# Fewer, wider stores of the last output tile and another order in the head of a fused attention and ELU kernel

## Chip, cores and metric

One core of a Trainium2 chip runs the whole kernel as one program. The metric is the device time of one execution in microseconds (us). Five engines work side by side, each through its own list of instructions in order: TensorE (PE, with its weight loads as PEld), VectorE (DVE), ScalarE (ACT), GpSimd (POOL) and SyncE (SP). SP and ACT also issue the DMA transfers; in the profile SP's transfers are queue q1 and ACT's are queue q10. Engines wait for each other, and for transfers, through semaphores.

## Reference

Inputs: `q`, `k`, `v` of shape (4 batches, 4 heads, 1088 positions, 32), two sketches `S1`, `S2` of shape (8, 32), and the weights `w_in` (128, 2048) and `w_out` (2048, 128), all given in 64-bit floats that the kernel rounds to float32 itself where it needs them (the sketches and the weights; `q`, `k`, `v` are float32).

```python
def phi(x):
    a = np.einsum('rd,bhsd->bhsr', S1, x)
    b = np.einsum('rd,bhsd->bhsr', S2, x)
    return np.einsum('bhsi,bhsj->bhsij', a, b).reshape(*x.shape[:-1], r * r)
q_p, k_p = phi(q), phi(k)
kv  = np.einsum('bhsf,bhsd->bhfd', k_p, v)
z   = np.sum(k_p, axis=2)
num = np.einsum('bhsf,bhfd->bhsd', q_p, kv)
den = np.einsum('bhsf,bhf->bhs', q_p, z)[..., None] + 1e-06
x   = (num / den) rearranged to (4352, 128)      # 4352 = 4 batches x 1088 positions, 128 = heads x 32
h   = x @ w_in
g   = np.where(h > 0, h, np.exp(np.minimum(h, 0)) - 1)
out = g @ w_out                                  # (4352, 128)
```

## The kernel before

**Tiling.** The 1088 positions of a batch are cut into 17 tiles of 64 (`NT` = 17, `KT` = 9), so there are 68 half tiles of 64 rows; a group `g` is 8 of them (512 columns), and the last of the nine groups has only 4. The 2048 hidden columns are 8 pairs `cp` of 2 x 128. The main loop walks over (group, pair): `mm1` makes two tiles of h on PE, `elu_a` (ACT, lines 787 and 789) and `elu_d` (DVE, line 795) make g, and `mm2`, `mm2_seven` or, for the last group, `mm2_last` adds the product with `w_out` up in PSUM. Between these steps the attention of the later batches is woven in by hand.

**Order.** The program is scheduled by hand: each engine runs its instructions in the order in which the Python code issues them. Only waits on semaphores come on top. Eight semaphores serve the DMA transfers in turn, so a transfer is issued once the one eight before it has landed.

**The head** (everything up to about 15 us) makes the first group's x from batch 0 as early as it can:

- Loads: `S1` on SP and `S2` on ACT (8 rows each), the first half of batch 0's keys (9 tiles) on SP and the second half (8 tiles) on ACT, the first 8 tiles of queries on SP, then on SP the first weights, `v` of batch 0 in two transfers, and the rest.
- `sps` (line 264) and `SXps` (`make_SXh`, line 250) on PE spread the two sketches; `Sab` (line 267, DVE) is `sps` times a mask of heads, the block matrix with which keys and queries are multiplied.
- `transp` (line 243) transposes keys and queries on DVE in 32 x 32 blocks: `kT` in four pieces (tiles 0 to 5 ahead of `Sab`, then 9 to 14, 5 to 9, 14 to 17), then `qT`.
- `KF(0)` (line 303) multiplies each `kT` tile with `Sab` into two PSUM tiles `abp`, in two streams, one for each half of the rows; two ACT copies (line 311) make `abk` of them. `q1_first` (line 478) does the same for the queries (`abqp`, copied to `abq` on ACT, line 482).
- The products of key features `kp` are made by POOL for tiles 0 to 4 (`KO_pool`, line 286) and by DVE for tiles 4 to 9 (`KO_first`, line 373).
- z: `z_tile` (line 381) sums over positions on PE (`zps`), `ZC` (line 403) copies to `zl` on ACT, `Z` (line 225) spreads on PE, and `Z_out` (line 412) masks on DVE into `SW`. `q1z_first` (line 490) multiplies the queries with it on PE (`zqp`), and `q2_den` (from line 565: `pw`, sum, reciprocal, `an`) and `q2_out` (line 582: `qp`, in two halves) finish the queries on DVE.
- `RA`, `RB`, `RC` round weights from 64-bit to 32-bit: `RA` (line 103) and `RC` (lines 116 to 129) on DVE, `RB` (line 108) on ACT.
- `KA(0)` (line 390) multiplies `v` with `kp` on PE; `KS_first` (lines 442 to 444) copies and transposes that; `q4_early` (line 594) transposes `qp` on PE, `q5_early` (line 601, `xps`) and the ACT copies at line 607 make `xg`, the x of a group.
- `keep_warm(n, cols)` (line 230) issues n products of constants into a PSUM tile that nobody reads. `KC` (line 399, `kvl`) copies kv out later, and line 225 is a helper that records most products, with `o` the result tiles of the first two groups.

**The tail.** `mm2_last` holds the last group's result with rows of the output on the partitions, in two PSUM tiles `ops[g][0]` and `ops[g][1]` (128 x 128 each, names `ol`). Tile i has half tile i on partitions 0 to 63 and half tile 2 + i on partitions 64 to 127. `fin_last` copies tile 0 on ACT and tile 1 on DVE (line 839) into `o`, and stores each half by itself (line 842): the lower half issued by SP, the upper by ACT. In `out`, the rows of one half tile lie 17 rows apart (64 rows of 512 bytes), and the two half tiles of a tile start two rows apart.

Of the kernel before, what the change touches and what calls it, by code (L numbers as in the profile page):

```python
# [22 lines left out]
def _ap(ap: bass.AP, free):  # L23
    return dataclasses.replace(ap, ap=[list(ap.ap[0])] + [list(x) for x in free])
# [3 lines left out]
def kernel(  # L28
# [21 lines left out]
    nc = tc.nc  # L50
# [7 lines left out]
    NT = S // 64  # L58
    KT = (NT + 1) // 2
# [12 lines left out]
    kT = [const.tile([FD, 2 * KT, 64], F32, name=f"kT{b}") for b in range(2)] * 2  # L72
    qT = [const.tile([FD, NT, 64], F32, name=f"qT{b}") for b in range(2)] * 2

    def load_hd(eng, x, src, b, t0, t1, c=slice(0, 2)):
        if (x, b) not in hd:
            hd[x, b] = work.tile([P, 2, NT, D], F32, name="hd_" + x, tag="hd_" + x)
        eng.dma_start(hd[x, b][:, c, t0:t1, :],
                      src[b].rearrange("h (a c t) d -> (h a) c t d", a=32, c=2)[:, c, t0:t1, :])
# [61 lines left out]
            eng.dma_start(S16[rs, :], src)  # L141
    load_hd(nc.sync, "k", k, 0, 0, KT)
    load_hd(nc.scalar, "k", k, 0, KT, NT)
    load_hd(nc.sync, "q", q, 0, 0, 8)
    warm = const.tile([R, 1], F32, name="warm")
    nc.vector.memset(warm[:], 0.0)
    nc.scalar.activation(warm[:], warm[:], EXP)
# [75 lines left out]
    def halves(dst, lhs, rhs, **kw):  # L223
        for u in range(2):
            nc.tensor.matmul(dst[64 * u:64 * u + 64], lhs[:, 64 * u:64 * u + 64], rhs, skip_group_check=True,  # L225
                             tile_position=(0, 64 * u), **kw)

    def keep_warm(n, cols=256):
        for i in range(n):
            nc.tensor.matmul(idle[:, :cols], some[:, :P], some[:, :cols], skip_group_check=True)  # L230
# [11 lines left out]
    def transp(dst, x, b, t0, t1):  # L242
        nc.vector.transpose(dst[b][:, t0:t1, :].rearrange("p t (a c) -> p c t a", c=2), hd[x, b][:, :, t0:t1, :])
# [4 lines left out]
    def make_SXh():  # L248
        xps = psum.tile([P, 512], F32, name="SXps", tag="aux")
        nc.tensor.matmul(xps[:, :FD], idr[:].rearrange("p x j -> p (x j)"), Sx[:].rearrange("p h d -> p (h d)"))  # L250
        nc.scalar.copy(SXh[:], xps[:, :FD])
        nc.gpsimd.tensor_mul(SXh[:].rearrange("p (h d) -> p h d", h=H), SXh[:].rearrange("p (h d) -> p h d", h=H),
                             _ap(hmask[:], [[1, H], [0, D]]))
# [9 lines left out]
    sps = psum.tile([P, 512], F32, name="sps", tag="aux")  # L263
    nc.tensor.matmul(sps[:, :2 * R], Sx[:].rearrange("p h d -> p (h d)"), ident[:, :2 * R])
    make_SXh()
    transp(kT, "k", 0, 0, 5)
    nc.vector.tensor_mul(Sab[:], _ap(sps[:, :2 * R], [[0, H], [1, 2 * R]]), _ap(bmask[:], [[1, H], [0, 2 * R]]))
    nc.gpsimd.tensor_copy(SW[:, :, :2, :].rearrange("p h x r -> p h (x r)"), Sab[:])

# [98 lines left out]
    def KO_first(t0, t1):  # L368
        half, o = divmod(t0, 5)
        n = t1 - t0  # L370
        a_ = kf_ps[half][:, 64 * o:64 * (o + n)].rearrange("p (m x r) -> p m x r", x=2, r=R)[:, :, 1, :]
        b_ = feats[0][:, 0, t0:t1].rearrange("p t h r -> p (t h) r")
        nc.vector.tensor_mul(feats[0, half][:, o:o + n].rearrange("p t h i j -> p (t h) i j"),
                             _ap(a_, list(a_.ap[1:]) + [[0, R]]), _ap(b_, [[R, n * H], [0, R], [1, R]]))
# [3 lines left out]
    def z_tile(b, ps, i):  # L378
        c = 32 * (i % 4)
        ab = feats[b]  # L380
        nc.tensor.matmul(ps[c:c + 32, R * R:R * R + H * R], ab[:, 0, i].rearrange("p h r -> p (h r)"),
                         ab[:, 1, i].rearrange("p h r -> p (h r)"), start=(b == 0 and i < 4), stop=(i >= KT - 4),
                         skip_group_check=True, tile_position=(0, c))
# [17 lines left out]
    def ZC(b, ps):  # L401
        zl = work.tile([P, H * R], F32, name="zl", tag="zl")
        nc.scalar.copy(zl[:], ps[:, R * R:R * R + H * R])
        return zl

    def Z(b, ps, zl):

        halves(ps[:, 96:128], SXh[:], zl[:])

    def Z_out(b, ps):  # L410
        z = wzs[b] = SW[:, :, 2, :] if b == 0 else work.tile([FD, H, R], F32, name="wz", tag="wz")[:]
        nc.vector.tensor_mul(z, ps[:, 96:128].rearrange("p (h i) -> p h i", h=H), _ap(bmask[:], [[1, H], [0, R]]))
# [21 lines left out]
    def Z_first():  # L434
        ps = psum.tile([P, 512], F32, name="zps", tag="h", bufs=4)
        for i in range(KT):
            z_tile(0, ps, i)
        return ps, ZC(0, ps)

    def KS_first():  # L440
        kd = work.tile([P, 2, R * R], F32, name="kd", tag="kd", bufs=1)
# [18 lines left out]
    def half_tile(g, k):  # L460
        return divmod(8 * g + k, NT)
# [11 lines left out]
    def q1_first():  # L473
        p = psum.tile([P, 512], F32, name="abqp", tag="aux")
        for i in range(4):
            for u in range(2):
                b, t = half_tile(0, 2 * i + u)
                nc.tensor.matmul(p[64 * u:64 * u + 64, i * 64:i * 64 + 64], qT[b][:, t, :],
                                 Sab[:].rearrange("p h y -> p (h y)"),
                                 skip_group_check=True, tile_position=(0, 64 * u))  # L480
        abw[0] = work.tile([P, H * 4, 2 * R], F32, name="abq", tag="abq", bufs=1)
        nc.scalar.copy(abw[0][:].rearrange("p (h t) y -> p h t y", h=H),
                       p[:, :256].rearrange("p (t h y) -> p h t y", t=4, h=H))

    def q1z_first():
        p = psum.tile([P, 512], F32, name="zqp", tag="h", bufs=4)
        for i in range(4):
            for u in range(2):
                b, t = half_tile(0, 2 * i + u)
                nc.tensor.matmul(p[64 * u:64 * u + 64, i * 32:i * 32 + 32].rearrange("p (h r) -> p h r", h=H),  # L490
                                 qT[b][:, t, :], SW[:, :, 2, :], skip_group_check=True, tile_position=(0, 64 * u))
        return p[:, :128].rearrange("p (t h r) -> p h t r", t=4, h=H)
# [341 lines left out]
    def fin_last():  # L834
        g, n = NQ - 1, qn[NQ - 1]
        o = work.tile([P, 2, P], F32, name="ol", tag="ol", bufs=1)
        rows = out.rearrange("(b y t) f -> b y t f", b=B, t=NT)
        for i, copy in enumerate((nc.scalar.copy, nc.vector.tensor_copy)):
            copy(o[:, i, :], ops[g][i][:])
            for u, eng in enumerate((nc.sync, nc.scalar)):  # L840
                b, t = half_tile(g, u * n + i)
                eng.dma_start(rows[b, :, t, :], o[64 * u:64 * u + 64, i])


    for t0, t1 in ((KT, KT + 5), (5, KT), (KT + 5, NT)):
        transp(kT, "k", 0, t0, t1)
    KF(0)
    transp(qT, "q", 0, 0, 8)
    zps, zl = Z_first()
    q1_first()  # L850
    KO_pool()
    KO_first(4, 5)
    KO_first(5, 7)
    Z(0, zps, zl)
    Z_out(0, zps)
    KO_first(7, KT)
    keep_warm(1, 96)
    zq = q1z_first()
    RA(0)
    q2_den(0, zq)  # L860
# [132 lines left out]
    for n in range(2, N + 2):  # L993
        if n < N:
            g, cp = steps[n]
# [26 lines left out]
        g, cp = steps[n - 2]  # L1022
# [5 lines left out]
        elif n > 2:  # L1028
            mm2(g, cp, cp == 0, cp == NP - 1)
            if cp == NP - 1:  # L1030
                fin1(g)
    fin_last()


# [27 lines left out]
```

## Time and profile before

| What | us |
|---|---|
| median of three runs | 267.58 |
| the three runs | 267.28, 267.58, 267.61 |
| the profiled execution: its own time | 267.61 |
| its span, first to last instruction | 265.83 |
| PE busy | 258.8 (97% of the span) |
| DVE, ACT, POOL busy | 187.8, 183.9, 159.8 |
| granted TensorE clock, mean | 1.000 of full speed |

All views count from the first instruction of the span. The time is 1.78 us longer than the span. The profile page has the busy times, the DMA queues with packets and bytes, and the chain of work that ended last, which is followed back from the last instruction. A timeline row gives start, length, engine, line, operation, output<-input, shapes and, in brackets, how long the engine was idle before it and who ended that; rows of one kind that follow each other closely are merged. In the records of DMA packets, each packet is one run of bytes that one of 16 DMA engines moved, without the name of that engine.

### The profile page before, as it was taken

How to read it: one execution, taken by the hardware profiler on the slowest of the kernel's cores; microseconds unless marked ns; L12 is line 12 of the kernel's file. 1: busy time of each engine (PE TensorE's matmuls, PEld its weight loads, DVE VectorE, ACT ScalarE, POOL GpSimd, SP SyncE). 2: the span in 40 equal slices, each digit the busy share in tenths (PEclk: the TensorE clock that was granted, in tenths of full speed). 3: DMA queues.
4: the chain of work that ended last, by engine and by line, in shares of the span. 5: the costliest groups of instructions: out<-in, count | busy, mean ns of one | idle time of the engine just before them, and what ended most of it. 6: DMA issues, size and time to landing. Idle time of an engine off the chain costs nothing.

```text
span 265.8 us, 7682 instructions
## 1 busy us (share of the span) xinstructions
PE 258.8 (97%) x3113; PEld 154.2 (58%) x3113; DVE 187.8 (71%) x347; ACT 183.9 (69%) x355; POOL 159.8 (60%) x233
## 2 busy tenths in 40 slices
PE   8799999999999999999999999999999999999994
PEld 7653233343334665668566666666766666666884
DVE  7899999996969796996557766654346444673652
ACT  2389978677566565786577777777777777777782
POOL 4400008204415985798858799898688888898300
PEclk9999999999999999999999999999999999999999
DMA  5999960010002300001100110001000100010011
GB/s 177 310 355 280 237 198 6 0 54 35 0 0 33 52 4 0 2 3 20 25 5 0 21 22 2 0 14 28 7 0 15 28 4 0 14 16 15 2 30 32
DMA packets 26402, 13.60 MB, mean 51 GB/s; under 512 B 19200, under 2 KB 24576, under 8 KB 26368
## 3 DMA queue, kind: packets, MB, share of 16 engines
q1 hardware_dynamic: 25920, 12.79, 19.1%
q8 instruction: 24, 0.39, 0.6%
q10 hardware_dynamic: 448, 0.33, 0.4%
q14 instruction: 10, 0.08, 0.1%
HBM read 10.88 MB, written 2.23 MB: 49 GB/s over the span
## 4 chain that ended last, share of the span: by engine, by line
PE 91%; ACT 4%; DMA 2%; SPq 1%; issue 1%; DVE 0%
PE h L225 42%; PE pb L726 16%; PE pa L726 12%; PE o L225 9%; PE ol L225 3%; DMA v<-in_v_dram 2%; PE kv L390 2%; PE h L644 1%; ACT e L789 1%; ACT e L787 1%; PE qps L644 1%; PE xps L601 1%; PE kfps L322 1%; PE qps L538 1%; PE kv L225 1%
## 5 line engine op out<-in xcount | busy, mean ns | idle before, releaser
L795 DVE SCALAR_TENSOR_TENSOR gg<-e,h 128x512 f32<-128x512 f32 (+1 forms) x144 | 92.3, 651 | 64.6 <-ACT e L789 63.2
L225 PE MATMUL h<-xg,W 128*64 128x512 f32 (+1 forms) x584 | 128.7, 563 | 0.0
L787 ACT ACTIVATE e<-h 128x512 f32<-128x512 f32 (+1 forms) x144 | 81.5, 566 | 50.4 <-PE h L225 47.9
L789 ACT ACTIVATE e<-e 128x512 f32<-128x512 f32 (+1 forms) x144 | 87.5, 607 | 4.4
L225 PEld LDWEIGHTS h<-xg,W 128*64 128x64 f32 x584 | 40.1, 137 | 47.4 <-issue 37.1
L706 POOL TENSOR_TENSOR tt<-gg 128x256 f32<-128x256 f32 x48 | 35.2, 733 | 16.4 <-DVE gg L795 15.9
L709 POOL TENSOR_TENSOR tt<-gg 128x256 f32<-128x256 f32 x48 | 35.4, 738 | 14.2 <-DVE gg L795 13.9
L711 POOL TENSOR_TENSOR tt<-gg,tt 128x256 f32<-128x256 f32 x48 | 36.5, 761 | 3.8
L710 POOL TENSOR_TENSOR tt<-tt,gg 128x256 f32<-128x256 f32 x48 | 35.2, 734 | 3.8
L726 PEld LDWEIGHTS pa<-gg,W 128*64 128x64 f32 x384 | 23.6, 137 | 22.8 <-issue 22.0
L225 PE MATMUL o<-gg,W 128*64 128x512 f32 x128 | 30.5, 598 | 0.2 <-ACT kvl L399 0.2
L726 PE MATMUL pa<-gg,W 128*64 128x128 f32 x384 | 29.5, 274 | 0.0
L726 PE MATMUL pb<-tt,SS 128*64 128x128 f32 x384 | 29.1, 273 | 0.0
L726 PEld LDWEIGHTS pb<-tt,SS 128*64 128x64 f32 x384 | 22.6, 137 | 0.0
L126 POOL TENSOR_TENSOR raw<-raw,tiny 128x512 f32<-128x512 f32 x1 | 1.0, 1042 | 30.4 <-DVE raw L121 30.4
L726 PE MATMUL pb<-gg,SS 128*64 128x128 f32 x192 | 18.7, 273 | 0.0
L726 PE MATMUL pb<-tt,W 128*64 128x128 f32 x192 | 18.6, 273 | 0.0
L726 PE MATMUL pa<-tt,SS 128*64 128x128 f32 x192 | 18.6, 273 | 0.0
L225 PEld LDWEIGHTS o<-gg,W 128*64 128x64 f32 x128 | 8.5, 136 | 16.2 <-issue 13.9
L726 PEld LDWEIGHTS pa<-tt,SS 128*64 128x64 f32 x192 | 12.1, 137 | 0.0
L726 PEld LDWEIGHTS pb<-tt,W 128*64 128x64 f32 x192 | 12.1, 137 | 0.0
L726 PEld LDWEIGHTS pb<-gg,SS 128*64 128x64 f32 x192 | 12.1, 137 | 0.0
(150 smaller groups left out, 242.2 us busy)
## 6 DMA issues: line engine op xcount, KB each, us to landing
raw<-in_moe_w_in_dram SPq DMA_DIRECT2D x8, 256.0 KB, 7.5
raw<-in_moe_w_out_dram SPq DMA_DIRECT2D x8, 256.0 KB, 7.0
hd_k<-in_k_dram SPq DMA_DIRECT2D x3, 544.0 KB, 8.3
hd_q<-in_q_dram SPq DMA_DIRECT2D x3, 544.0 KB, 9.1
v<-in_v_dram SPq DMA_DIRECT2D x4, 288.0 KB, 8.8
out_dram<-ob SPq DMA_DIRECT2D x72, 16.0 KB, 1.5
v<-in_v_dram SPq DMA_DIRECT2D x4, 256.0 KB, 7.7
out_dram<-ob SPq DMA_DIRECT2D x16, 32.0 KB, 1.7
```

What stands on the lines that cost most here:

```text
L225: nc.tensor.matmul(dst[64 * u:64 * u + 64], lhs[:, 64 * u:64 * u + 64], rhs, skip_group_check=True, tile_position=(0, 64 * u), **kw)
L322: nc.tensor.matmul(ps[g2][32 * c:32 * c + 32, :32 * KT], Sxp[r].rearrange("p x c r -> p (x c r)"), kT[b][r, u * KT:u * KT + KT, 32 * w:32 ...
L390: nc.tensor.matmul(kv[32 * h:32 * h + 32, :R * R], vt[b][:, (h * KT + i) * D:(h * KT + i + 1) * D], kp[i // 5][:, i % 5, h].rearrange("p i ...
L644: nc.tensor.matmul(ps[w][s * r:s * r + s, 64 * k:64 * (k + m)], lhs, qpT[g, i][rows, o + 2 * k:o + 2 * (k + m), f, :], start=(f == 0 and j ...
L706: nc.gpsimd.tensor_tensor(t[:, 0], b12, b11, op=SUB)
L709: nc.gpsimd.tensor_tensor(t[:, 2], b22, b12, op=SUB)
L710: nc.gpsimd.tensor_tensor(t[:, 1], t[:, 2], b11, op=ADD)
L711: nc.gpsimd.tensor_tensor(t[:, 3], b21, t[:, 1], op=SUB)
L726: nc.tensor.matmul(bank[64 * u:64 * u + 64, P * col:P * col + P], lhs, rhs[:, u], start=(first and i in (0, 3)), stop=last, skip_group_che ...
L787: nc.scalar.activation(e, hs[g, cp][c][:, :n], RELU, scale=-1.0)
L789: nc.scalar.activation(e, e, EXP, scale=-1.0)
L795: nc.vector.scalar_tensor_tensor(gs[g, cp][:, c, :n], es[g, cp][:, c, :n], -1.0, hs[g, cp][c][:, :n], op0=ADD, op1=MAX)
```

## The change

Head: q's first load is split into two transfers, c = 0 on SP and c = 1 on ACT (behind ACT's half of the keys). The first piece of `kT` is transposed behind `Sab` in place of ahead of it, and a filler product of 224 columns stands on PE behind `SXps`. z's sums, copy, spread and mask are issued together, after `q1_first` and after all of `KO_first`; `KO_first(5, 7)` and `KO_first(7, KT)` become one instruction `KO_first(5, KT)`. The filler after z has 160 columns in place of 96.

Tail: each of the two last tiles is stored by one transfer of 128 rows, tile 0 issued by ACT behind its copy, tile 1 by SP behind the copy on DVE. On the DRAM side the transfer is written as (u, y, f) = 2 x 64 x 128: u steps from a half tile to the one two rows on, y over its 64 rows.

The function that loads half heads takes a slice of c already:

```python
    def load_hd(eng, x, src, b, t0, t1, c=slice(0, 2)):
        ...
        eng.dma_start(hd[x, b][:, c, t0:t1, :],
                      src[b].rearrange("h (a c t) d -> (h a) c t d", a=32, c=2)[:, c, t0:t1, :])
```

```diff
     load_hd(nc.sync, "k", k, 0, 0, KT)
     load_hd(nc.scalar, "k", k, 0, KT, NT)
-    load_hd(nc.sync, "q", q, 0, 0, 8)
+    load_hd(nc.sync, "q", q, 0, 0, 8, slice(0, 1))
+    load_hd(nc.scalar, "q", q, 0, 0, 8, slice(1, 2))
...
     make_SXh()
-    transp(kT, "k", 0, 0, 5)
+    keep_warm(1, 224)
     nc.vector.tensor_mul(Sab[:], ...)
...
     def Z_first():
         ps = psum.tile([P, 512], F32, name="zps", tag="h", bufs=4)
         for i in range(KT):
             z_tile(0, ps, i)
-        return ps, ZC(0, ps)
+        zl = ZC(0, ps)
+        Z(0, ps, zl)
+        Z_out(0, ps)
+        keep_warm(1, 160)
...
     def fin_last():
...
-        for i, copy in enumerate((nc.scalar.copy, nc.vector.tensor_copy)):
+        for i, (copy, eng) in enumerate(((nc.scalar.copy, nc.scalar), (nc.vector.tensor_copy, nc.sync))):
             copy(o[:, i, :], ops[g][i][:])
-            for u, eng in enumerate((nc.sync, nc.scalar)):
-                b, t = half_tile(g, u * n + i)
-                eng.dma_start(rows[b, :, t, :], o[64 * u:64 * u + 64, i])
+            b, t = half_tile(g, i)
+            eng.dma_start(rows[b, :, t:t + n + 1:n, :].rearrange("y u f -> u y f"), o[:, i])
...
-    for t0, t1 in ((KT, KT + 5), (5, KT), (KT + 5, NT)):
+    for t0, t1 in ((0, 5), (KT, KT + 5), (5, KT), (KT + 5, NT)):
         transp(kT, "k", 0, t0, t1)
     KF(0)
     transp(qT, "q", 0, 0, 8)
-    zps, zl = Z_first()
     q1_first()
     KO_pool()
     KO_first(4, 5)
-    KO_first(5, 7)
-    Z(0, zps, zl)
-    Z_out(0, zps)
-    KO_first(7, KT)
-    keep_warm(1, 96)
+    KO_first(5, KT)
+    Z_first()
     zq = q1z_first()
```

## The prediction

> **What bounds the kernel now.** I read the chain of waits first, in two stretches, because the diff touches only the first 10 us and the last 4 us. In each row: start in us, length in us, what.
>
> ```profile
> 3.90 6.48 DMA v<-in_v_dram
> 10.38 0.14 issue
> 10.51 1.25 PE kv L390 x72
> ...
> 20.64 1.24 PE xps L601 x16
> 21.88 0.63 ACT xg L607 x2
> ...
> 30.42 0.27 ACT kvl L399
> 30.68 0.04 issue
> 30.73 1.50 PE o L225 x5
> ```
>
> To see: up to 10.38 us the end is set by the landing of `v`, not by the head's arithmetic; then PE and ACT pass the chain to and fro until 30.68, and from there PE is nearly unbroken. DVE, whose order the diff changes most, is nowhere on it. Next, the timeline of DVE in the head (start, length, engine, line, operation):
>
> ```profile
> 5.00 0.18 DVE L267 TENSOR_TENSOR Sab<-sps,bmask 128x64 f32<-128x64 f32 x1
> 7.08 1.11 DVE L373 TENSOR_TENSOR kp<-abp,abk 128x256 f32<-128x256 f32 x2 [0.17 <-ACT abk L311]
> 8.61 0.19 DVE L412 TENSOR_TENSOR SW<-zps,bmask 128x32 f32<-128x32 f32 x1 [0.42 <-PE zps L225]
> 8.71 0.68 DVE L373 TENSOR_TENSOR kp<-abp,abk 128x512 f32<-128x512 f32 x1
> 9.63 0.29 DVE L565 TENSOR_TENSOR pw<-abq,zqp 128x128 f32<-128x128 f32 x1
> ```
>
> The mask product of z (SW) starts at 8.61; `pw` follows 1.02 us later, through q1z. From 8.61 DVE has no idle stretch worth naming before 24.85, where it waits 0.34 us for ACT. So a late SW shifts DVE for 16 us; the question is who waits for DVE.
>
> Third, the timeline of the tail:
>
> ```profile
> 261.87 0.27 ACT L839 COPY ol<-ol 128x128 f32<-128x128 f32 x1 [1.06 <-PE ol L225]
> 262.16 1.19 SPq L842 DMA_DIRECT2D out_dram<-ol  x2
> 262.16 1.46 ACTq L842 DMA_DIRECT2D out_dram<-ol  x2
> 262.31 0.29 DVE L839 COPY ol<-ol 128x128 f32<-128x128 f32 x1 [1.04 <-PE ol L225]
> ```
>
> Issues start at 262.16 and 262.80 on SP, 262.16 and 262.81 on ACT. In the packet records SP's two transfers write at 263.36-263.66 and 264.00-264.30, ACT's at 263.63-263.93 and 264.28-264.59. The last instruction ends at 265.83, 1.24 us after the last packet, all of it waiting and closing.
>
> Fourth, the DMA queues (queue: packets, MB, share of 16 engines), once for 1.6:1.9, when only the sketches `S1` and `S2` are in flight, and once for 263.2:263.7, where q1 (SP) holds just the first output store:
>
> ```profile
> DMA packets 32, 0.00 MB, mean 14 GB/s; under 512 B 32, under 2 KB 32, under 8 KB 32
> ...
> q10 hardware_dynamic: 16, 0.00, 4.1%
> q1 hardware_dynamic: 16, 0.00, 4.0%
> ```
>
> ```profile
> q1 hardware_dynamic: 80, 0.03, 27.2%
> ```
>
> To see: a store of 64 rows leaves 80 packets, 64 of data and 16 completion records of 4 bytes: 16 engines took part. A sketch of 8 rows leaves 16, 8 of data and 8 completions: 8 engines. And both sketches used the same 8: the records pair off, such as data at 1.686 and completion at 1.698 on q1, then data at 1.710 and completion at 1.721 on q10, eight times over with the same 12 ns steps. So where the outermost count is below 16, it sets how many engines share a transfer, and two queues can land on the same ones.
>
> **The tail, step by step.** Four transfers become two. The built instruction has SBUF rows 128 x 128 on one side, and on the DRAM side the outermost count is 2 (2 x 64 x 128; the list of instructions shows 2x64x128 where it showed 64x128). The change removes one issue on SP (0.54) and one on ACT (0.81), each behind another, and SP's only one now waits for the DVE copy. No row here has unequal counts on its two sides. The bounds are 16 engines (the 64-row stores) and 2 (the destination's outer count); I take 2, nearest to the 8-row sketches, the only row with an outer count under 16.
>
> Rate of one engine: the share of 27.2% of 16 engines over 0.5 us is 2.18 us of packet time, less 16 x 9 ns of completions, over 64 packets: 32 ns per 512 bytes while 16 engines contend. The last engine of that store, alone by then, started packets at 263.554, .579, .604 and .628: 25 ns each. With two engines at work I take 25 and keep 32 for the range.
>
> The ACT store is issued at 262.16 as before; first packet 1.20 us later (SP's delay, both times): about 263.4. The DVE copy ends at 262.60, so SP issues at about 262.62 and is ready at 263.8, when the ACT store is a quarter done on the same two engines. Each engine has 64 + 64 packets: 128 x 25 ns = 3.2 us, done at 266.6 in place of 264.59: **+2.0 us**. At 32 ns: 4.1 us, done at 267.5, +2.9. On two separate pairs: 263.8 + 1.6 = 265.4, +0.85. What follows the last packet keeps its 1.24 us. Nothing hides this: only waiting comes after.
>
> The Trainium skill speaks on both sides. Its page DMA: Bandwidth & Descriptors, section Rules for kernel authors, advises one 128-partition transfer over two of disjoint halves, which is what the change does. The same page, section Why a DMA increments its semaphore by 16 and not by 1, says the count of engines is the largest number up to 16 that divides the slowest dimension of both sides: 2 here, which no run here shows yet. The page's Specifications give about 27 GiB/s per engine, by which 64 KB would take, as an estimate, 2.3 us and the sum would be +1.1; the 25 ns of the trace make 20 GB/s, and the trace's figure is the one used.
>
> **The head, step by step.**
> - q's first load in two halves, the second on ACT. ACT's table load (1.28 us at 2.06) moves behind a 0.6 us issue; ACT is idle from 3.55 to 5.21, which covers it. If that cover were gone, SXh's copy would be late by up to 0.6. SP's issue of `v` stays where it is: SP's early issues take 0.60 to 0.69 whether they hold 128 or 256 rows. The same bytes lie ahead of `v`, on engines that are over 90% busy from 3.5 us on. Landing of `v`: unchanged, give or take 0.2. One more load moves the semaphores by one place; each then waits for a transfer issued eight before, for `v` a sketch landed at 1.8.
> - First key transpose behind Sab. Sab no longer sits behind it (5.00 to about 4.92), but the transpose (0.51; 0.43 to the next) then runs at 5.15, and every key and query transpose ends 0.36 later. KF's second stream on PE starts 0.46 later, and the ACT copies abk with it: 7.08 and 7.55 for 6.62 and 7.09.
> - The 224 column filler on PE, two passes (a 256 column pair spans 0.60): 5.0 to 5.6, ahead of KF's new start at 5.70. Hidden.
> - abqp now precedes zps on PE, abq precedes zl on ACT; Z is ready near 9.05 for 8.5. KO_first(5, 9) is one DVE instruction of 0.69 + 256 x 2 x 1.04 ns = 1.22 us (1.04 ns per element, from 425 ns for 256 and 692 for 512) from 7.95 to 9.17. SW starts at about 9.1 for 8.61: **+0.5 on DVE**, up to 0.7 if Z is last. RA(0) now runs under q1z.
> - The 160 column filler lies in q1z's wait for SW. Hidden.
>
> Who waits: the first qp half would end at 12.15, its transpose starts at 12.70 behind the kv chain; the second at 12.76 for 13.13; the next group's second half at 19.6 for 19.74. The first loss is at 21.71, where o needs W from L129 (ends 21.51, then 22.0): PE loses 0.35. But o at 30.73 waits for ACT's kvl, while PE could have started at 30.35 (its pairs step by 0.43 after 29.92): 0.38 of slack takes it back, and ACT's chain from 21.88 to 30.68 needs nothing that comes late. DVE itself recovers at 24.85 (0.34) and 29.84 (0.46). Net 0, with 0.3 to 0.5 if SW is 0.7 late or `v` lands later, and -0.2 if `v` lands earlier. I take **+0.1**.
>
> Sum against the profiled execution (span 265.83, time 267.61, 0.03 over the median of 267.58): 267.6 + 2.0 + 0.1 = **269.7 us**.
>
> **Rivals.**
> - *All 16 engines serve the 128 rows* (not slower). The place is the last two stores; it decides if a store leaves 16 completion records. Then SP's store starts writing at 263.8, twice the 0.30 us of a 64-row store: done at 264.4 for 264.59, -0.15; with the head 267.6. For it: the source has 128 rows. Against: the sketches' 8 completions.
> - *Two engines each, on different pairs*: +0.85 + 0.1, 268.6. Against it: the paired sketches.
> - *The head's slack does not hold*: 0.5 lost before 31 us, with the forecast tail 270.1. For it: 0.38 covers 0.35 only just.
>
> **How the numbers follow.** Forecast 0.70, all engines 0.15, separate pairs 0.07, head not absorbed 0.08. The forecast's own range is 269.3 (head -0.2, packets a little quicker) to 270.7 (32 ns). The range 268.4 to 270.7 takes in separate pairs and the lost slack and leaves out the first rival and a little above. A change within 0.2% (0.54 us) can't be told from none here; the first rival falls there, rarely beyond it: faster 0.03, same 0.12, slower 0.85.
>
> **What would show it.** Right: the tail's DMA window shows 132 packets for two stores, 128 of data and 4 completions, spread over some 3 us at a share near 2/16; the last landing near 266.6; SW near 9.1; kv still at 10.5; o at 30.7 unmoved. Wrong: 160 packets and an end of packets before 264.6, or kv moved by more than 0.2.

## The result, and the profile after

The changed kernel takes 270.37 us (median of six runs, 269.95 to 270.84); the kernel before took 267.48 beside it (six runs, 267.21 to 267.74). The ratio is 1.011, interval 1.0096 to 1.0125: 2.9 us slower, 0.7 above the forecast of 269.7 and inside its range. The profiled execution took 270.53 us with a span of 268.70, for 267.61 and 265.83 before. One execution below, of `tail_64x2` (274.08 us), ran at a lower granted clock than its others and is not counted.

Those 2.87 us of span lie in two places. The step of `o` that started at 30.73 now starts at 31.49 and ACT's copy of the last tile starts at 262.57 in place of 261.87, so 0.7 us come from the head. From the end of that copy to the end of the last packet it is 4.65 us in place of 2.45, so 2.2 come from the tail. The step of `o` in the timelines of PE, before and after:

```profile
30.73 1.94 PE L225 MATMUL o<-gg,W 128*64 128x512 f32 x8 [0.21 <-ACT kvl L399]
31.49 1.89 PE L226 MATMUL o<-gg,W 128*64 128x512 f32 x8
```

The timeline of the tail after the change (start, length, engine, line, operation):

```profile
262.57 0.27 ACT L843 COPY ol<-ol 128x128 f32<-128x128 f32 x1 [1.06 <-PE ol L226]
262.87 0.66 ACTq L845 DMA_DIRECT2D out_dram<-ol  x1
263.01 0.29 DVE L843 COPY ol<-ol 128x128 f32<-128x128 f32 x1 [1.04 <-PE ol L226]
263.33 0.63 SPq L845 DMA_DIRECT2D out_dram<-ol  x1
```

The DMA queues in the window 264.1:267.6, which holds both stores (queue: packets, MB, share of 16 engines):

```profile
DMA packets 260, 0.13 MB, mean 37 GB/s; under 512 B 4, under 2 KB 260, under 8 KB 260
...
q10 hardware_dynamic: 130, 0.07, 7.1%
q1 hardware_dynamic: 130, 0.07, 6.2%
```

To see: the issues are as short as before, but each store left 128 packets of data and 2 completion records of 4 bytes ("under 512 B 4"), so two engines carried it, if one engine leaves one completion as in the prediction's reading. The two shares add up to 13.3% of 16 engines, 2.1 engines. The packet records show ACT's store from 264.16 to 265.97 and SP's from 265.94 to 267.48. SP's store was issued at 263.33 and wrote nothing for 2.6 us, until ACT's was done: the same two engines, one store after the other. In SP's store packets start 11.9 ns apart on average, so about 24 ns apart on one of two engines; in ACT's, where some packets took up to 107 ns, 14.1 ns and 28. Over both it is 26 ns for each engine.

In the head, the chain of waits no longer starts with `v`:

```profile
2.07 5.25 DMA hd_q<-in_q_dram
7.34 0.72 DVE qT L244
8.06 0.14 issue
8.20 0.70 PE abqp L482 x16
8.92 0.37 ACT abq L486
9.29 0.13 ACT zl L404
9.43 0.14 issue
9.56 0.31 PE zps L226 x4
...
10.34 0.61 PE zqp L494 x16
10.98 0.30 DVE pw L569
```

And the timeline of DVE over the same stretch, with the idle time before a row and who ended it in brackets:

```profile
4.92 1.51 DVE L244 STREAM_TRANSPOSE kT<-hd_k 128x320 f32<-128x320 f32 x4
7.34 0.71 DVE L244 STREAM_TRANSPOSE qT<-hd_q 128x512 f32<-128x512 f32 x1 [0.91 <-DMA hd_q<-in_q_dram]
...
9.98 0.19 DVE L413 TENSOR_TENSOR SW<-zps,bmask 128x32 f32<-128x32 f32 x1 [0.49 <-PE zps L226]
```

Before, the same transpose of q in the timeline of DVE:

```profile
6.24 0.67 DVE L243 STREAM_TRANSPOSE qT<-hd_q 128x512 f32<-128x512 f32 x1
```

To see: the half of q that ACT issues at 2.07 lands only at 7.32. DVE sits idle for 0.91 us before it transposes, and everything that follows is one line of waits: abqp, abq, zl, Z, SW at 9.98 in place of 8.61. Before, qT started at 6.24 and waited for nothing. The chain goes on from `pw` through DVE to the first `o`, which waits 0.40 us for DVE's W and starts at 22.86 in place of 21.71; from there PE is unbroken. KA(0)'s `kv` started at 10.86, for 10.51: by then PE was held by zqp (10.27 to 10.93) and no longer by `v`.

### The profile page after: what moved, and what is told of

It reads as the page before. It is cut to its first block, busy times and chain, and to the rows that moved or that the text cites. A ratio compares the mean times of both kernels' runs of the same rounds, so it can differ in the third digit from the quotient of the medians.

```text
span 268.7 us, 7682 instructions
## 1 busy us (share of the span) xinstructions
PE 259.3 (97%) x3115; PEld 154.1 (57%) x3115; DVE 187.3 (70%) x346; ACT 184.0 (68%) x355; POOL 159.8 (59%) x233
## 4 chain that ended last, share of the span: by engine, by line
PE 90%; DVE 4%; DMA 2%; issue 1%; ACTq 0%; ACT 0%; DVEq 0%
PE h L226 42%; PE pb L730 16%; PE pa L730 12%; PE o L226 11%; PE ol L226 3%; DMA hd_q<-in_q_dram 2%; PE kv L391 1%; PE h L648 1%; PE qps L648 1%; DVE qp L586 1%; PE kfps L323 1%; PE qps L542 1%; PE kv L226 1%; DVE qT L244 1%; DVE raw L121 0%
## 5 line engine op out<-in xcount | busy, mean ns | idle before, releaser
L730 PEld LDWEIGHTS pa<-gg,W 128*64 128x64 f32 x384 | 23.6, 137 | 22.8 <-issue 22.1
```

Source lines behind the costliest of these rows:

```text
L730: nc.tensor.matmul(bank[64 * u:64 * u + 64, P * col:P * col + P], lhs, rhs[:, u], start=(first and i in (0, 3)), stop=last, skip_group_che ...
```

## The experiments

Twelve kernels ran, in three groups, each beside the kernel before on the same chip (medians 267.41, 267.41 and 267.54). Differences below are between medians; the ratios with their 95% intervals go by means.

**Which half of the change costs what.** The change with the head put back, and with the tail put back:

```diff
 tail_only: the kernel before, with
-            for u, eng in enumerate((nc.sync, nc.scalar)):
-                b, t = half_tile(g, u * n + i)
-                eng.dma_start(rows[b, :, t, :], o[64 * u:64 * u + 64, i])
+            b, t = half_tile(g, i)
+            eng.dma_start(rows[b, :, t:t + n + 1:n, :].rearrange("y u f -> u y f"), o[:, i])
 head_only: all other lines of the change
```

> The head of before, the tail of the change. Theory (each wide store runs on two engines, the same two): packets of both stores in 130 + 130 records, from about 263.4 to 266.7 us, the end 2.2 us later than before: about 269.7 us. Rival (the late head explains most of the 2.9 us): under 268.2 us.

> The head of the change, the tail of before. Theory (the head costs what the tail does not): 0.7 us over before, about 268.2 us, with the first main product o at about 22.9 us for 21.7. Rival (the head's delay is taken back by slack and the tail is all of it): within 0.2 us of before, 267.5.

`tail_only`: 269.57 us (269.23 to 269.87), ratio 1.0072 [1.0051, 1.0093], +2.16. `head_only`: 268.16 (267.32 to 269.37), ratio 1.0018 [0.9996, 1.0039], +0.75. The two add up to 2.91, and the whole change cost 2.89. The interval of `head_only` takes in 1 and its runs lie 2 us apart, so by itself it says little; the change less `tail_only`, each against the kernel before beside it, is 2.89 - 2.16 = 0.73 and gives the same size from another pair. `tail_only` has the same packets as the change, from its window 263.3:266.9:

```profile
DMA packets 260, 0.13 MB, mean 36 GB/s; under 512 B 4, under 2 KB 260, under 8 KB 260
```

Its SW started 0.48 late, `o` at 21.71 0.30 late and `o` at 30.73 0.04 early, so a late SW was absorbed here, in an execution whose head varied by itself. The fourteen profiles say when that is so. In twelve of them the step of `o` starts 21.5 to 21.7 us after SW. In the other two, before (22.1) and `tail_64x4` (21.8), it waits for ACT's kvl, and starts 20.2 us after `kv` (10.51 and 10.30). The later of the two paths, SW + 21.5 or `kv` + 20.2, fits all fourteen to 0.2 us. So the slack behind SW, 0.6 us in the profile of before, is there only while `v` makes `kv` that late. What is lost at this step stays lost: in the seven profiles with the tail of before, the execution's time less the start of `o` is 236.7 to 237.0.

The chain of `head_only`'s profiled execution shows the late q at its largest, q landing at 8.37 (its time was 269.37, the slowest of its runs):

```profile
2.06 6.31 DMA hd_q<-in_q_dram
8.37 0.02 issue
8.40 0.72 DVE qT L244
```

**Is it the outermost count?** Stores of 64 rows as before, but with the outermost count of the DRAM side made 2 by nesting the rows (columns of the last group's x, `q5_out`, are ordered to match), and stores of 128 rows with an outermost count of 64:

```diff
 tail_64x2:
-    nc.scalar.copy(x[:, :2 * n].rearrange("p (k w s) -> p w k s", w=2, s=64)[:, w],
-                   ps[w][:, :n].rearrange("p (k s) -> p k s", s=64))
+    nc.scalar.copy(x[:, :2 * n].rearrange("p (k w a b) -> p w k a b", w=2, a=2, b=32)[:, w],
+                   ps[w][:, :n].rearrange("p (k b a) -> p k a b", a=2, b=32))
-    eng.dma_start(rows[b, :, t, :], o[64 * u:64 * u + 64, i])
+    eng.dma_start(rows[b, :, t, :].rearrange("(b a) f -> a b f", a=2), o[64 * u:64 * u + 64, i])
 tail_16: the tail of the change, with
-    nc.scalar.copy(x[:, :2 * n].rearrange("p (k w s) -> p w k s", w=2, s=64)[:, w],
+    nc.scalar.copy(x[:, :2 * n].rearrange("p (k s w) -> p w k s", w=2, s=64)[:, w],
-    eng.dma_start(rows[b, :, t:t + n + 1:n, :].rearrange("y u f -> u y f"), o[:, i])
+    eng.dma_start(rows[b, :, t:t + n + 1:n, :], o[:, i])
```

> Before, with its four stores of 64 rows and the same issues, but rows interleaved by two, so that the outermost count on the DRAM side is 2 with 32 rows inside. Theory (the outermost count sets the engines): 66 records per store, four stores one after the other on the same two engines, 128 packets of 23.5 ns each: packets end near 266.5 us, the time about 269.4. Rival (a store of 128 rows or 64 KB is slow in itself, whatever its outermost count): as before, 267.5.

> The head of before, two stores of 128 rows as in the change, but partitions ordered (row, half) in place of (half, row), so that the outermost count on the DRAM side is 64. One copy earlier writes the last group's columns with a step of two. Theory (the outermost count sets the engines): 80 or 144 records per store on 16 engines, packets end near 264.4 us, the time 0.1 to 0.3 us under before: about 267.3. Rival (a store of 128 rows is slow in itself): as the tail of the change, 269.7.

`tail_64x2`: 270.06 (269.54 to 271.43, seven runs), ratio 1.0087 [1.0052, 1.0122], +2.65. `tail_16`: 267.23 (266.86 to 267.76), ratio 0.9977 [0.9956, 0.9999], -0.18. The queues of the two, windows 263.3:267.0 and 263.7:264.7:

```profile
DMA packets 264, 0.13 MB, mean 35 GB/s; under 512 B 8, under 2 KB 264, under 8 KB 264
```

```profile
DMA packets 288, 0.13 MB, mean 131 GB/s; under 512 B 32, under 2 KB 288, under 8 KB 288
...
q10 hardware_dynamic: 144, 0.07, 23.1%
q1 hardware_dynamic: 144, 0.07, 22.6%
```

Four stores with 8 completions use two engines each, two stores with 32 use sixteen each. In these kernels the number of stores and the rows in each do not matter to it, the outermost count on the DRAM side does: 4.72 us from the copy to the last packet in `tail_64x2`, 2.13 in `tail_16`, where the same 128 KB have all started by 264.62. `tail_64x2` lies 0.5 over `tail_only`, though its packets end only 0.08 later after the copy and its profiled execution took 269.90 (269.87 for `tail_only`). From the start of `o` at 30.74 and 30.69 to the end, these two executions take 239.16 and 239.18, so the tail does not hold that half microsecond; what does is open. `tail_16` is the fastest kernel here, but by 0.07% between medians, so it is level with the kernel before rather than clearly ahead: with sixteen engines one store of 128 rows does what two of 64 did.

**How the time scales.** An outermost count of 4 in all four stores; and tile 0 stored as before with tile 1 as in the change:

```diff
 tail_64x4: as tail_64x2, with a=4, b=16
+    eng.dma_start(rows[b, :, t, :].rearrange("(b a) f -> a b f", a=4), o[64 * u:64 * u + 64, i])
 tail_one:
+    if i == 0:
+        ...two stores of 64 rows, as before
+    else:
+        b, t = half_tile(g, i)
+        nc.sync.dma_start(rows[b, :, t:t + n + 1:n, :].rearrange("y u f -> u y f"), o[:, i])
```

> Before, with its four stores of 64 rows, rows interleaved by four: outermost count 4 with 16 rows inside. Theory: 68 records per store, the four stores one after the other on four engines, 64 packets of 23.5 ns each: packets end near 265.1 us, 0.4 to 0.6 us over before, 267.9. Rival (only a count of 2 hurts, or the interleaved writes do): 267.4, or as with the count of 2, 270.1.

> Before, with tile 0 stored as before in two stores of 64 rows and tile 1 by one store of 128 rows with outermost count 2, issued by SP. Theory (two engines at 23.5 ns a packet): its packets from 264.0 to 265.6 us, 1.0 us over before, 268.4. Rival (a wide store costs only because the two queue behind each other): 267.4 to 267.6.

`tail_64x4`: 268.09 (267.76 to 268.82), ratio 1.002 [1.0006, 1.0034], +0.55. `tail_one`: 268.46 (268.13 to 269.49), ratio 1.0026 [1.0004, 1.0047], +0.92. The queues of `tail_64x4` in 263.0:266.0 hold four stores with 4 completions each:

```profile
DMA packets 272, 0.13 MB, mean 44 GB/s; under 512 B 16, under 2 KB 272, under 8 KB 272
```

From copy to last packet: 4.64 us with 128 packets on each engine (`tail_only`), 3.50 with 64 for the one wide store (`tail_one`, whose first packet comes 0.58 later after the copy), 2.98 with 64 (`tail_64x4`). The step from 64 to 128 packets is (4.64 - 2.98) / 64 = 26 ns each, beside the 25 of the prediction.

**What in the head costs.** First the parts: the change with q's first load whole again, and the kernel before with one part of the new head each.

```diff
 q_whole: the change, with
-    load_hd(nc.sync, "q", q, 0, 0, 8, slice(0, 1))
-    load_hd(nc.scalar, "q", q, 0, 0, 8, slice(1, 2))
+    load_hd(nc.sync, "q", q, 0, 0, 8)
 q_split_only: the kernel before, with these lines the other way round
 z_order_only: the kernel before, with
-    zps, zl = Z_first()
     q1_first()
     ...
-    KO_first(5, 7)
-    Z(0, zps, zl)
-    Z_out(0, zps)
-    KO_first(7, KT)
-    keep_warm(1, 96)
+    KO_first(5, KT)
+    Z_first()          # sums, copy, spread, mask, keep_warm(1, 160)
 kt_order_only: the kernel before, with
-    transp(kT, "k", 0, 0, 5)
+    keep_warm(1, 224)
...
-    for t0, t1 in ((KT, KT + 5), (5, KT), (KT + 5, NT)):
+    for t0, t1 in ((0, 5), (KT, KT + 5), (5, KT), (KT + 5, NT)):
```

> The change, with q's first load again in one transfer on SP. Theory (the half on ACT lands late, and the head's 0.7 us is that): qT starts near 6.4 us, SW at 9.1 to 9.4, o at 30.7 as before; the time 269.6, as with the tail alone. Rival (z's later place in the order is the cost): 270.3, as the change.

> Before, with only q's first load split between SP and ACT. Theory: the half on ACT lands at 7.3 us or later, qT waits for it 0.9 us or more, SW comes 0.5 to 1.0 later, and what is over 0.5 is lost: 0.1 to 0.5 us over before, 267.5 to 267.9. Rival (z's order alone): 267.4, within 0.1 of before.

> Before, with only z's steps moved behind all of KO_first and behind q1, and the filler of 160 columns. Theory (late q): SW 0.1 to 0.5 later, within the slack, the time within 0.15 us of before, 267.4. Rival (z's order is the cost): 0.5 to 0.7 us over before, 268.0.

> Before, with only the first key transposes behind Sab and the filler of 224 columns on PE. Both theories: every transpose ends 0.1 to 0.4 us later, SW as much, within the slack: within 0.15 us of before, 267.4.

| Kernel | median us (lowest to highest) | ratio to before | SW starts in its profile |
|---|---|---|---|
| `q_whole` | 269.81 (269.56 to 270.58) | 1.0091 [1.0078, 1.0104] | 8.90 |
| `q_split_only` | 267.47 (266.95 to 268.63) | 1.0003 [0.9992, 1.0015] | 8.64 |
| `z_order_only` | 267.38 (267.12 to 267.97) | 0.9999 [0.9990, 1.0008] | 8.90 |
| `kt_order_only` | 267.25 (266.96 to 268.05) | 0.9996 [0.9988, 1.0005] | 9.46 |

The new order costs nothing that can be told, in either part, and the split alone costs nothing either; yet taking the split out of the change gives back 0.49 of the head's 0.73 (2.89 - 2.40, each against the kernel before beside it), with ratios whose intervals just overlap, [1.0096, 1.0125] and [1.0078, 1.0104]. So split and order seem to cost only together; the next two kernels show it more clearly. The SW of one profile is not that of a median: `kt_order_only`'s profiled execution took 267.70, 0.45 over its median, and PE was late in it, KF starting at 6.24, and full speed in the clock records first at 6.07. In `q_split_only`'s profile q's second half landed at 6.2 and DVE waited for nothing, so that trace does not show whether the old order would have borne a late q.

Then the queue against the number of transfers: the changed head with the tail of before, q whole on ACT, and q in two halves that SP issues both.

```diff
 head_q_act:
+    load_hd(nc.scalar, "q", q, 0, 0, 8)
 head_q_two_sp:
     load_hd(nc.sync, "q", q, 0, 0, 8, slice(0, 1))
+    load_hd(nc.sync, "q", q, 0, 0, 8, slice(1, 2))
```

> The head of the change and the tail of before, with all of q's first load issued by ACT behind its half of the keys. Theory (what queues on ACT lands late): q lands at 8.5 us or later, qT waits over 2 us for it, and the head costs 1.5 to 2.5 us: 269 to 270. Rival (the late half has another cause): no worse than the head of the change, 268.2.

> The head of the change and the tail of before, with q's two halves both issued by SP, one behind the other. Theory (the late landing comes from ACT's queue, not from there being two transfers): q lands near 6 us, nothing waits for it; within 0.2 us of before, 267.5. Rival (two transfers, or the shifted semaphores, are the cost): as the head of the change, 268.2.

`head_q_act`: 269.62 (269.55 to 272.28), ratio 1.0097 [1.0060, 1.0134], +2.08. `head_q_two_sp`: 267.56 (267.29 to 268.29), ratio 1.0000 [0.9987, 1.0014], +0.02. In the chain of `head_q_act`:

```profile
2.06 6.55 DMA hd_q<-in_q_dram
8.61 0.02 issue
8.63 0.72 DVE qT L243
```

and in the tile view of `hd_q` in `head_q_two_sp`, the time from issue to landing:

```profile
DMA to landing us min/median/max: 3.9/3.9/4.0
```

So it is the queue and not the number of transfers: the same two halves land 3.9 to 4.0 us after issue when both are SP's, and the new order then costs 0.02 (interval -0.13% to 0.14%). On ACT's queue half of q takes 4.1 us (`q_split_only`), 5.2 (the change) and 6.3 (`head_only`), with the same loads in all three, and all of q takes 6.6; the new order then costs 0.75 for half of q and 2.08 for all of it. The profiled execution of `head_q_two_sp` is no picture of its median: it took 268.29, the longest of its twelve, and had SW at 9.87 and the step of `o` at 31.33 with q on time. There KF started only at 6.14 and ran past 8 us; the clock records show full speed first at 7.26. Why the load is late on ACT's queue is argued, not shown. The packet records are suggestive: 90% of ACT's packets have started by 5.3 to 5.4 us in the change, in `head_only` and in `q_split_only` alike, and the last few start at 6.52, 7.19 and 5.66, at the time when SP's queue, which has the first weights right behind q, ends those (6.65, 7.51, 6.30). It would fit engines that serve the two queues in turn, so that a small load on one queue waits among the large loads of the other. No run here kept the weights back to try it, and in `head_q_act` the last packet of q starts at 7.71, long after the last of the first weights (6.04), so these weights alone don't account for it.

## Why the prediction was right and where it was wrong

- **Two engines by the destination's count: right.** 2 completions per store, as forecast, also for 64 rows (`tail_64x2`), with 4 for a count of 4 and 16 for 64 rows on one side and 128 on the other. The rule that the prediction quoted from the Trainium skill, page DMA: Bandwidth & Descriptors, section Why a DMA increments its semaphore by 16 and not by 1, is what these counts show. The advice of its section Rules for kernel authors, one transfer of 128 partitions in place of two halves, is given there for halves that spread over all 16 engines. With the rows as the change orders them, where the one transfer does not, following it cost 2.16 us; with the rows ordered as in `tail_16` the time is level with before (-0.18). My "132 packets for two stores" was a slip in adding: 256 of data and 4 completions.
- **The tail's +2.0: right, 2.16 measured.** 25 ns per packet was 26 over both stores (24 in SP's, 28 in ACT's, where some packets took up to 107 ns), so 3.2 us of packets were 3.3. The stores did not overlap as I had pictured, but on the same two engines that changes no sum. The rest is at the front: the first packet came 1.29 us after the issue for 1.20.
- **Separate pairs and all engines: both fell.** The second store began when the first ended, and no store of the change left 16 completions.
- **The new order of the head: right by itself.** `z_order_only`, `kt_order_only` and, with both parts, `head_q_two_sp` cost nothing that can be told. The slack before `o` at 30.73 is there in the profile it was read from: 0.83 of lateness in SW (`tail_16`) leaves 0.42 at that step, 1.37 (the change) leaves 0.76, 2.43 (`head_only`) leaves 1.83. About 0.4 to 0.6 is free against that profile, for 0.38 in the prediction, and what goes beyond it is lost one for one. What I did not see is that it is slack against `v`: with `kv` early, as in `q_split_only` (9.47), the step of `o` comes at 30.16, and none is left.
- **The step that failed: "q's first load in two halves".** I priced ACT's issue (hidden, right) and the landing of `v` (which held up nothing more), and never asked when the second half itself lands on its new queue. The next step, "abqp now precedes zps on PE", then took q as on time: before, qT ran at 6.24 without a wait, and the new order puts z behind it, so that q's delay of about a microsecond reaches SW. That turned the head's +0.1 into 0.73 to 0.75, of which the split explains 0.49 by `q_whole` and nearly all by `head_q_two_sp`. The rival "the head's slack does not hold" named the place, with 0.5 for the price and another cause; the fallback in the text, ACT's table load, played no part.
- **The signs.** SW came at 9.98 for about 9.1, the step of `o` at 31.49 for 30.7, and `kv` at 10.86 for 10.5, which is more than the 0.2 that I had named as a sign of being wrong. That sign was right about the head.
- **Luck in the range.** Its upper end of 270.7 stood for packets of 32 ns. They took 26, and the late q filled that room, so that 270.37 lies inside the range is in part luck.

## What to carry to other kernels

Count the completion records of a transfer (here the packets of 4 bytes) when you have widened it: an outermost count of 2 on the DRAM side left it two engines, and a store at the very end has nothing to hide behind, while the same rows in an order with an outermost count of 64 cost nothing. When a load is moved to another queue, price its landing there, with all that the other queue has in flight, and not just the issue. And price edits together where one puts work behind the result of another: here neither the split nor the order showed a cost alone, and together they cost 0.75 us. And ask of a slack which other path makes it, and whether that path is as late in every execution.

## What the runs showed of the hardware that was not expected

- Two stores from two queues on the same two engines ran one after the other: SP's, issued 0.46 us after ACT's, wrote its first packet 2.6 us after its issue, when ACT's last was out. The Trainium skill, page DMA: Bandwidth & Descriptors, section Queues, rings and completion order, says that an engine takes turns between its queues at the boundaries of packets, and means by a packet a group of typically 9 to 17 descriptors, at most 64, not one run of bytes as in these records. Here each engine wrote all 64 runs of ACT's store before SP's first. In `tail_64x2`, with 32 runs per engine and store, the queues took turns store by store: SP, ACT, SP, ACT. No run here shows what sets where a turn ends.
- With nothing else in flight, one engine wrote 512 bytes every 23.5 ns, 21.8 GB/s (second store of `tail_only`), and every 24.8 ns in the wide store of `tail_one`.
- The head varies from execution to execution by more than some of its parts cost. KF's 36 products with the same operands took 1.82 us in the profile of before and 2.50 in that of `tail_16`, where the clock records show full speed first at 4.72 and at 7.30:

```profile
5.24 1.82 PE L303 MATMUL abp<-Sab,kT 128*64 128x64 f32 x36
```

```profile
5.39 2.50 PE L303 MATMUL abp<-Sab,kT 128*64 128x64 f32 x36
```

  And `kv` started between 9.65 (`tail_one`) and 10.52 (`tail_64x2`) with the loads of before. Both reach the time through the step of `o`, KF by way of SW and `v` by way of `kv`, whichever is later.
